# Top-k attention and an MLP on one core: values taken a step later and ahead of the scores, first MLP products four blocks to a PSUM bank

## The chip, the core and the metric

The kernel runs on one core of one Trainium2 chip. The metric is the device time of one execution in microseconds; the time before is 1606.17 us, the median of 3 runs (1605.85 to 1606.31). The engines are named as in the profile: PE (TensorE, matrix products), PEld (its weight loads), DVE (VectorE), ACT (ScalarE), POOL (GpSimd) and SP (SyncE, which issues the DMAs).

## The reference

```
# q, k, v: 8 batches, 8 heads, 576 rows, 64 columns, float32
scores = (q @ k.T) / sqrt(64)
kth = np.partition(scores, -32, axis=-1)[..., -32:-31]
scores = np.where(scores >= kth, scores, -1e9)
attn = softmax(scores)                       # 1e-9 is added to the sum
x = (attn @ v) laid out as (8 * 576, 8 * 64) # 4608 tokens x 512
h = x @ w_in                                 # 512 x 2048
g = h if h >= 1;  0 if h <= -1;  (h + 1)**2 / 4 between
out = g @ w_out                              # 2048 x 512
```

## The kernel before

**Tiles.** Attention goes in 144 steps. A step is 128 query rows of two heads: its scores are two tiles of 576 columns each. The 4608 tokens are 36 chunks of 128, and a chunk's 512 input columns (`xT`) are complete after four steps. The steps that hold the last 64 rows of two batches put four heads into one step.

**One step on the engines.** PE multiplies queries by keys (`scores`, L285), ACT copies the result to `s` (L287). DVE finds the 32nd largest of each row over several passes (`weights`, `first_top`, L297 to L388); ACT takes the exponential (L323); DVE masks and sums it (L386). POOL divides by the sum (`divide`, L339). In the late part of the kernel `move_w` (L412) then transposes the weights by DMA: ACT copies the 4-byte weights apart into 2-byte halves (L416), SP writes these to DRAM (L418) and reads them back with a transposing DMA (L419) into `wT`. PE multiplies `wT` by the values (`values`, L433 and L441), and ACT copies that product from PSUM into `xT` (L446, L448). In the first steps, while the MLP weights are still being converted (`convert_piece`), and in the last two, `transpose_w` (L395) does the transposing on PE instead, with a diagonal matrix `diag` that ACT makes.

**The MLP.** `mlp` cuts a chunk's work into items and appends them to the list `pending`. `hidden(x)` multiplies `GROUP` = 2 blocks of 128 hidden columns (16 matmul instructions) into one PSUM tile `ph`; ACT reads it twice (L470 to `r`, L477 to `g`), POOL makes the activation out of the two in three instructions (L482 to L484). `final(f)` adds one block's product with `w_out` to `py` (two instructions of 512 columns). The finals of a group come `LAG` = 4 groups behind its hidden item. After the last final ACT copies `py` to `y` (L492) and SP writes it out. The finals that are left over from a chunk are mixed between the first hidden items of the next.

**PSUM.** The tag `ph` has three buffers, shared by `ph` and the values' `po`; the tag `a` has two, shared by the scores `sp` and by all transposes (`pk`, `pq`, `pw`); `py` has one.

**The order.** PE, DVE, ACT and POOL each run their instructions in the order in which the program's planner emits them; SP's order isn't set by hand. The planner (L661 to L725) goes through the steps; step `m` has seven slots. In the late part, slot 0 emits the division of step `m-1`; slot 1 the transposes of queries and keys to come; slot 2 `move_w(m-1)`; slot 3 the maximum and first exponential of step `m+1` and a check of the MLP weights (`inspect`, ACT Sign); slot 4 the second exponential, `begin_at(m+2)` (the scores of step `m+2`) and `values_until(m-1)`, which is the values of step `m-2`. At the end of every slot `advance` takes items from `pending` as far as a budget `due` goes. An item costs one unit for each 128-column product of a hidden block (8 for a pair) and 4 for a final; the budget per step is `share`, about 32 units, and it is lowered so that the list doesn't run empty before the next chunk's values come (L669 to L673). An item whose weights aren't converted yet blocks the list.

Of the kernel before, what the change touches and what calls it, by code (L numbers as in the profile page):

```python
# [10 lines left out]
F32 = mybir.dt.float32  # L11
# [3 lines left out]
AF = mybir.ActivationFunctionType  # L15
ALU = mybir.AluOpType
# [8 lines left out]
def kernel(  # L25
# [10 lines left out]
    nc = tc.nc  # L36
    B, H, S, D = q.shape
# [13 lines left out]
    BANK = 512  # L51
    NK = DM // P
    NF = DFF // P
    GROUP = 2
    LAG = 4
    SCALE = float(D) ** -0.5

    const = ctx.enter_context(tc.tile_pool(name="const", bufs=1))
# [103 lines left out]

    def inspect_piece(pool, i):

        _, hi = words_of(pool, i, 2)
        for x in range(2):
            sign = pool.tile([P, WC], F32, name="sign", bufs=1)
            nc.scalar.activation(sign, hi.bitcast(F32), AF.Sign, bias=tiny[:, x:x + 1],  # L168
                                 accum_out=signs[:, x, i:i + 1])


    def run(ctx, paired):
# [24 lines left out]
        def load_queries(b, t):  # L197
            if t < NT:
                q_in = stage.tile([P, H, D], F32, name="q_in", bufs=2)
                nc.sync.dma_start(out=q_in, in_=whole(q, b)[:, :, t, :])  # L200
            else:
                q_in = stage.tile([TL, H, D], F32, name="q_tl", bufs=1)
                nc.sync.dma_start(out=q_in, in_=q[b, :, SM:S, :].rearrange("h p d -> p h d"))
            return q_in

# [124 lines left out]
        def divide(st):  # L330
            rz = att.tile([P, 2], F32, name="rz")
            nc.vector.reciprocal(rz, st["z"])
            if st["by_tensor"]:
                st["rz"] = diag = (late or words).tile([P, 2, P], F32, name="diag", bufs=1)
                for i in range(2):
                    nc.scalar.activation(diag[:, i, :], ident, AF.Copy, scale=rz[:, i:i + 1])
            else:
                for i in range(2):
                    nc.gpsimd.tensor_scalar(st["e"][:, i, :], st["e"][:, i, :], rz[:, i:i + 1], 1.0, ALU.mult, ALU.mult)  # L339
            if paired:  # L340
                m, seconds, kth = st["m"], st["seconds"], st["kth"]
                nc.gpsimd.tensor_tensor(out=excess[:, 2 * m:2 * m + 2], in0=seconds[:, 8:9 + SPLIT:SPLIT], in1=kth[:, LAST:7:-SPLIT],
                                        op=ALU.subtract)
# [50 lines left out]

        def transpose_w(st):  # L395
            w = st["e"]
            st["wT"] = wT = (late or words).tile([P, BLOCKS, P], F32, name="wT", bufs=2 if late else 1)
            pt = ps.tile([P, 2, NT, P], F32, name="pw", tag="a", bufs=2)
            for i in range(2):
                for c in range(NT):  # L400
                    nc.tensor.matmul(pt[:, i, c, :], w[:, i, main(i)][:, c * P:(c + 1) * P], st["rz"][:, i, :],  # L401
                                     start=True, stop=True)
            for i in range(2):
                nc.scalar.copy(wT[:, i * (NT + 1):i * (NT + 1) + NT], pt[:, i])
            pt = ps.tile([P, P], F32, name="pwt", tag="a", bufs=2)
            for i in range(2):
                nc.tensor.matmul(pt[i * TL:(i + 1) * TL, :], w[:, i, tail(i)], st["rz"][:, i, :], start=True, stop=True)
            nc.scalar.copy(wT[:, NT], pt)
# [1 line left out]


        def move_w(st):  # L412
            st["wT"] = wT = late.tile([P, BLOCKS, P], F32, name="wT", bufs=2)
            halves = late.tile([P, 2, 2 * S], U16, name="halves")
            for i in range(2):
                nc.scalar.copy(halves[:, :, i * S:(i + 1) * S], st["e"][:, i, :].bitcast(U16).rearrange("p (k t) -> p t k", t=2))  # L416
            rows = dram.tile([P, 2, 2 * S], U16, name="rows")
            nc.sync.dma_start(out=rows, in_=halves)  # L418
            nc.sync.dma_start_transpose(wT.bitcast(U16), rows.rearrange("p t k -> (p t) k"))  # L419
# [37 lines left out]
        def mlp(xT, rows, pool, last):  # L457
            gs, group = {}, 1 if last else GROUP
            py = []

            def hidden(x):
                ph = ps.tile([P, group, P], F32, name="ph", tag="ph", bufs=3)
                for i in range(group):
                    f = x * group + i
                    for kk in range(NK):
                        nc.tensor.matmul(ph[:, i], w_in[:, kk, f * P:(f + 1) * P], xT[:, kk],  # L466
                                         start=(kk == 0), stop=(kk == NK - 1))

                r = pool.tile([P, GROUP, P], F32, name="r", bufs=2)[:, 0:group]
                nc.scalar.activation(r, ph, AF.Relu, bias=half, scale=0.5)  # L470
                gs[x] = g = pool.tile([P, GROUP, P], F32, name="g", bufs=2 * LAG)[:, 0:group]
                if last:
                    nc.vector.tensor_scalar(g, ph, -1.0, 0.0, ALU.add, ALU.max)
                    nc.scalar.activation(r, r, AF.Square)
                    nc.vector.scalar_tensor_tensor(out=g, in0=r, scalar=1.0, in1=g, op0=ALU.min, op1=ALU.add)
                    return
                nc.scalar.activation(g, ph, AF.Relu, bias=minus, scale=1.0)  # L477
                if converted < n_pieces and x % 2:
                    nc.scalar.activation(r, r, AF.Square)
                    nc.gpsimd.tensor_scalar(r, r, 1.0, 0.0, ALU.min, ALU.max)  # L480
                else:
                    nc.gpsimd.tensor_scalar(r, r, 1.0, 0.0, ALU.min, ALU.max)  # L482
                    nc.gpsimd.tensor_tensor(out=r, in0=r, in1=r, op=ALU.mult)  # L483
                nc.gpsimd.tensor_tensor(out=g, in0=r, in1=g, op=ALU.add)  # L484

            def final(f):
                if f == 0:
                    py.append(ps.tile([P, DM], F32, name="py", tag="py", bufs=1))
                nc.tensor.matmul(py[0], gs[f // group][:, f % group], w_out[:, f, :], start=(f == 0), stop=(f == NF - 1))  # L489
                if f == NF - 1:  # L490
                    y = (late or words).tile([P, DM], F32, name="y", bufs=2)
                    nc.scalar.copy(y, py[0])  # L492
                    for p0, p1, dst in rows:
                        nc.sync.dma_start(out=dst, in_=y[p0:p1])

            behind = []
            while pending and pending[-1][3]:
                behind.insert(0, pending.pop())  # L500
            for x in range(NF // group + LAG):
                if x < NF // group:
                    pending.append((NK * group, needed(x * group + group - 1, False), partial(hidden, x), False))
                if x < LAG:
                    for _ in range(min(GROUP, len(behind))):
                        pending.append(behind.pop(0)[0:3] + (False,))
                else:
                    for f in range((x - LAG) * group, (x - LAG + 1) * group):
                        pending.append((DM // P, needed(f, True), partial(final, f), x >= NF // group))
# [151 lines left out]
        for m in range(n + 2):  # L661
# [6 lines left out]

            share, left = (total - spent) / (n + 2 - m), sum(x[0] for x in pending)  # L669
            for r in sorted(ready):  # L670
                if r + 3 > m and r >= valued:
                    share = min(share, left / (r + 3 - m))
                    left += NK * NF + NF * DM // P  # L673
            top_k, parts = None, [0] * SLOTS
            if m < n:
# [7 lines left out]
            for slot in range(SLOTS):  # L683
# [3 lines left out]
                if m < n and converted < n_pieces:  # L687
                    if slot in now_converting:
                        convert(now)
                elif slot == 3 and late is not None:  # L690
                    if m % 2:
                        inspect()
                    elif paired:
                        load(late, inspected, 2)
                if slot == 1 and 1 <= m <= n and state[m - 1]["by_tensor"]:
                    pe_time = max(pe_time, done[m - 1] + 2.0) + 1.0
                    transpose_w(state[m - 1])
                    ready_at[m - 1] = pe_time + 1.8
                if slot == 2 and 1 <= m <= n and not state[m - 1]["by_tensor"]:
                    move_w(state[m - 1])  # L700
                    ready_at[m - 1] = done[m - 1] + 14.0
                if slot == 2 and m == n and paired:
                    judge(ps, att)
                if slot == 2 and (early or m == first_late or m >= n - 1):
                    values_until(m)
                if m == 0 and slot in (1, 2):
                    next(first)
                if slot == 4:
                    begin_at(m + 2)
                    if not early:  # L710
                        values_until(m - 1)
                if slot == (6 if early else 1):
                    queries(m + 3)
                    if m < n and prep is None and next_keys < B and steps[m][0] == next_keys - 1 and steps[m][1] >= 1:
# [61 lines left out]
```

## Time and profile before

The profiled execution took 1610.32 us, and its span, from the first to the last instruction, is 1608.5 us: 1.8 us lie around the span. It is 4.15 us above the median of the three timed runs. The mean granted TensorE clock is 0.977.

| what | number |
|---|---|
| PE busy | 1514.0 us of 1608.5 |
| DVE busy | 1422.1 us (88%) |
| ACT busy | 1140.4 us (71%) |
| POOL busy | 943.3 us (59%) |
| hidden products, matmul instructions | 4608 |
| final products, matmul instructions | 1152 |
| reads of `ph` by ACT, 256 columns (L470, L477) | 280 + 280, 475 and 471 ns each |
| copies of `halves` by ACT (L416) | 260, 1153 ns each |
| transposing DMAs (L419) | 130 |

The engines work side by side, so only the time of the one that everything waits for can be taken off the end. The modelled ends of matmuls overlap the next one's start; how long a piece of PE work takes is therefore read from its start to the start of the piece behind it.

### The profile page before, as it was taken

What the parts mean: (1) busy time and instruction counts of PE and PEld (TensorE: products, weight loads), DVE (VectorE), ACT (ScalarE), POOL (GpSimd) and SP (SyncE); (2) the same over time, 40 slices, a digit from 0 to 9 for tenths busy, and PEclk for the clock granted to TensorE, in tenths of its full rate; (3) what the DMA queues carried; (4) which work ended last, traced back from release to release, by engine and by line L of the source; (5) the groups of instructions that cost most, each with busy time, mean ns of one, the idle gap of its engine ahead of it and who ended that gap; (6) DMA issues with size and microseconds to landing.
All of it is one profiled execution on the core that took longest, in us unless ns stands there. A gap on an engine that the chain in (4) does not pass through costs nothing.

```text
span 1608.5 us, 32395 instructions
## 1 busy us (share of the span) xinstructions
PE 1514.0 (94%) x10925; PEld 1080.7 (67%) x10925; DVE 1422.1 (88%) x4443; ACT 1140.4 (71%) x2308; POOL 943.3 (59%) x1376
## 2 busy tenths in 40 slices
PE   5587999999999999999999999999999999999988
PEld 4465676777667776777667767766666667666665
DVE  7999889999998998999999998999898998889932
ACT  5677567777777767777768877776677776677632
POOL 5766466666555665655556666555555665556640
PEclk7798999999999999999999999999999999999999
DMA  9433246565465556665565545655565555544410
GB/s 252 132 96 110 72 130 174 157 158 153 133 174 161 154 143 173 161 150 145 145 172 159 160 133 157 172 143 140 135 174 146 142 142 130 145 131 126 123 51 16
DMA packets 439056, 227.92 MB, mean 142 GB/s; under 512 B 393056, under 2 KB 401248, under 8 KB 438880
## 3 DMA queue, kind: packets, MB, share of 16 engines
q1 hardware_dynamic: 438880, 225.75, 51.8%
q8 instruction: 88, 1.44, 0.4%
q14 instruction: 88, 0.72, 0.1%
HBM read 62.91 MB, written 86.11 MB: 93 GB/s over the span
## 4 chain that ended last, share of the span: by engine, by line
PE 71%; ACT 13%; POOL 4%; DVE 4%; DMA 4%; issue 3%; SPq 1%; POOLq 0%; ACTq 0%; DVEq 0%
PE ph L466 27%; PE py L489 24%; PE sp L285 8%; PE po L433 7%; ACT halves L416 3%; ACT e L323 3%; DMA wT<-rows 2%; ACT s L287 2%; ACT sign L168 2%; PE pw L401 1%; POOL e L339 1%; POOL r L483 1%; PE po L441 1%; ACT r L470 1%; POOL g L484 1%
## 5 line engine op out<-in xcount | busy, mean ns | idle before, releaser
L466 PEld LDWEIGHTS ph<-xT,w_in 128*128 128x128 f32 x4608 | 554.4, 192 | 118.3 <-issue 79.8
L466 PE MATMUL ph<-xT,w_in 128*128 128x128 f32 x4608 | 576.1, 278 | 14.8 <-ACT xT L446 12.9
L489 PE MATMUL py<-w_out,g 128*128 128x512 f32 x1152 | 558.6, 601 | 7.3 <-ACT y L492 7.1
L482 POOL TENSOR_SCALAR r<-r 128x256 f32<-128x256 f32 x276 | 150.7, 546 | 526.5 <-ACT r L470 526.1
L307 DVE MATCH_REPLACE8 more<-tops,more 128x288 f32<-128x288 f32 x864 | 375.2, 437 | 0.0
L416 ACT COPY halves<-e 128x1152 uint16<-128x1152 uint16 x260 | 288.0, 1153 | 112.7 <-POOL e L339 111.5
L470 ACT ACTIVATE r<-ph,half 128x256 f32<-128x256 f32 (+1 forms) x296 | 139.0, 470 | 241.1 <-PE ph L466 227.9
L489 PEld LDWEIGHTS py<-w_out,g 128*128 128x128 f32 x1152 | 193.5, 191 | 137.0 <-issue 131.2
L386 DVE SCALAR_TENSOR_TENSOR e<-s,kth,e 128x577 f32<-128x577 f32 x288 | 249.2, 900 | 0.1
L484 POOL TENSOR_TENSOR g<-r,g 128x256 f32<-128x256 f32 x280 | 219.6, 784 | 22.0
L323 ACT ACTIVATE e<-s,nmax 128x576 f32<-128x576 f32 x288 | 217.4, 770 | 4.7
L339 POOL TENSOR_SCALAR e<-e,rz 128x576 f32<-128x576 f32 x260 | 218.6, 851 | 0.0
L483 POOL TENSOR_TENSOR r<-r 128x256 f32<-128x256 f32 x276 | 201.5, 730 | 23.0
L300 DVE TENSOR_TENSOR more<-s 128x576 f32<-128x576 f32 x144 | 114.9, 798 | 109.0 <-ACT s L287 108.6
L287 ACT ACTIVATE s<-sp 128x576 f32<-128x576 f32 x288 | 169.2, 638 | 4.5 <-PE sp L285 4.2
L285 PE MATMUL sp<-kT,qT 64*128 64x288 f32 x1024 | 162.0, 433 | 9.9 <-ACT kT L244 9.0
L285 PEld LDWEIGHTS sp<-kT,qT 64*128 64x128 f32 x1024 | 89.6, 188 | 98.9 <-issue 29.1
L433 PE MATMUL po<-wT,v_in 128*64 128x128 f32 x2048 | 145.9, 282 | 10.3 <-DMA wT<-rows 7.9
L433 PEld LDWEIGHTS po<-wT,v_in 128*64 128x64 f32 x2048 | 113.4, 139 | 60.5 <-issue 37.5
L477 ACT ACTIVATE g<-ph,minus 128x256 f32<-128x256 f32 x280 | 131.8, 471 | 0.0
L348 DVE MAX8 tops<-more 128x8 f32<-128x288 f32 x288 | 125.4, 442 | 0.0
L300 DVE TENSOR_TENSOR less<-s 128x576 f32<-128x576 f32 x144 | 117.4, 815 | 0.0
(92 smaller groups left out, 1528.2 us busy)
## 6 DMA issues: line engine op xcount, KB each, us to landing
rows<-halves SPq DMA_DIRECT2D x130, 576.0 KB, 2.8
raw<-in_moe_w_out_dram SPq DMA_DIRECT2D x52, 256.0 KB, 2.8
raw<-in_moe_w_in_dram SPq DMA_DIRECT2D x48, 256.0 KB, 2.9
k_in<-in_k_dram SPq DMA_DIRECT2D x64, 128.0 KB, 3.2
q_in<-in_q_dram SPq DMA_DIRECT2D x32, 256.0 KB, 3.3
v_in<-in_v_dram SPq DMA_DIRECT2D x8, 1024.0 KB, 5.9
out_dram<-y SPq DMA_DIRECT2D x32, 256.0 KB, 3.0
kT<-in_moe_w_in_dram SPq DMA_DIRECT2D x16, 256.0 KB, 4.6
```

The lines of the kernel that those rows point to most:

```text
L285: nc.tensor.matmul(o[:, a0 - c0:a1 - c0], qT[d, g, :], kT[d, g, k0:k0 + a1 - a0], start=True, stop=True)
L300: nc.vector.tensor_tensor(out=x, in0=s[:, :, 0:SH], in1=s[:, :, SH:S], op=op)
L307: nc.vector.match_replace(out=st["rest"][:, i, :], in_to_replace=eight(st["tops"], i, r - 8), in_values=src[:, i, :], imm_value=LOWEST)
L323: nc.scalar.activation(e[:, i, :], s[:, i, :], AF.Exp, bias=nmax[:, i:i + 1])
L339: nc.gpsimd.tensor_scalar(st["e"][:, i, :], st["e"][:, i, :], rz[:, i:i + 1], 1.0, ALU.mult, ALU.mult)
L386: nc.vector.scalar_tensor_tensor(out=st["all"][1][:, i, :], in0=st["all"][0][:, i, :], scalar=last[i], in1=st["all"][1][:, i, :], op0=ALU. ...
L416: nc.scalar.copy(halves[:, :, i * S:(i + 1) * S], st["e"][:, i, :].bitcast(U16).rearrange("p (k t) -> p t k", t=2))
L433: nc.tensor.matmul(po[j * D:(j + 1) * D], v_in[:, h, c, :] if c < NT else v_tl[0][:, h, :], wT[:, block(j, c)], start=(c == 0), stop=(c == ...
L466: nc.tensor.matmul(ph[:, i], w_in[:, kk, f * P:(f + 1) * P], xT[:, kk], start=(kk == 0), stop=(kk == NK - 1))
L483: nc.gpsimd.tensor_tensor(out=r, in0=r, in1=r, op=ALU.mult)
L484: nc.gpsimd.tensor_tensor(out=g, in0=r, in1=g, op=ALU.add)
L489: nc.tensor.matmul(py[0], gs[f // group][:, f % group], w_out[:, f, :], start=(f == 0), stop=(f == NF - 1))
```

## The change

The change has two parts and a number of smaller edits that fit them into the memory.

The first is in the MLP. `GROUP` becomes 4 and `LAG` 2: a hidden item is four blocks (16 units), its PSUM tile is a whole bank, and ACT reads it 512 columns at a time. POOL still works on 256 columns, in two rounds of three instructions. The list `pending` has half as many hidden items, each with the conversion of four blocks' weights as its condition.

The second is in the order. In the late part `begin_at(m+2)` goes from slot 4 to slot 2, and in front of it come the values of step `m-3` (`values_until(m-2)`). `move_w(m-1)` goes from slot 2 to slot 3. The planner's shares and due times are adapted (`r + 4`, 15.0), and `wT` has three buffers in place of two.

The smaller edits: the check of the weights writes its unused signs over the piece's low words, and its loads have one buffer; the 64-row queries share the buffers of the others; `diag` shares the tag of `halves`; `y` has one buffer in place of two.

```diff
-    GROUP = 2
-    LAG = 4
+    GROUP = 4
+    LAG = 2
...
-        _, hi = words_of(pool, i, 2)
+        lo, hi = words_of(pool, i, 1)
         for x in range(2):
-            sign = pool.tile([P, WC], F32, name="sign", bufs=1)
-            nc.scalar.activation(sign, hi.bitcast(F32), AF.Sign, bias=tiny[:, x:x + 1],
+            nc.scalar.activation(lo.bitcast(F32), hi.bitcast(F32), AF.Sign, bias=tiny[:, x:x + 1],
                                  accum_out=signs[:, x, i:i + 1])
...
-                q_in = stage.tile([TL, H, D], F32, name="q_tl", bufs=1)
+                q_in = stage.tile([TL, H, D], F32, name="q_tl", tag="q_in", bufs=2)
...
-                st["rz"] = diag = (late or words).tile([P, 2, P], F32, name="diag", bufs=1)
+                st["rz"] = diag = (late or words).tile([P, 2, P], F32, name="diag", tag="halves", bufs=1)
...
-            st["wT"] = wT = late.tile([P, BLOCKS, P], F32, name="wT", bufs=2)
+            st["wT"] = wT = late.tile([P, BLOCKS, P], F32, name="wT", bufs=3)
...
-                if converted < n_pieces and x % 2:
+                squared = converted < n_pieces and x % 2
+                if squared:
                     nc.scalar.activation(r, r, AF.Square)
-                    nc.gpsimd.tensor_scalar(r, r, 1.0, 0.0, ALU.min, ALU.max)
-                else:
-                    nc.gpsimd.tensor_scalar(r, r, 1.0, 0.0, ALU.min, ALU.max)
-                    nc.gpsimd.tensor_tensor(out=r, in0=r, in1=r, op=ALU.mult)
-                nc.gpsimd.tensor_tensor(out=g, in0=r, in1=g, op=ALU.add)
+                for c in range(0, group, 2):
+                    rh, gh = r[:, c:c + 2], g[:, c:c + 2]
+                    nc.gpsimd.tensor_scalar(rh, rh, 1.0, 0.0, ALU.min, ALU.max)
+                    if not squared:
+                        nc.gpsimd.tensor_tensor(out=rh, in0=rh, in1=rh, op=ALU.mult)
+                    nc.gpsimd.tensor_tensor(out=gh, in0=rh, in1=gh, op=ALU.add)
...
-                    y = (late or words).tile([P, DM], F32, name="y", bufs=2)
+                    y = (late or words).tile([P, DM], F32, name="y", bufs=1)
...
-                if r + 3 > m and r >= valued:
-                    share = min(share, left / (r + 3 - m))
+                if r + 4 > m and r >= valued:
+                    share = min(share, left / (r + 4 - m))
...
-                        load(late, inspected, 2)
+                        load(late, inspected, 1)
...
-                if slot == 2 and 1 <= m <= n and not state[m - 1]["by_tensor"]:
+                if slot == 3 and 1 <= m <= n and state[m - 1] is not None and not state[m - 1]["by_tensor"]:
                     move_w(state[m - 1])
-                    ready_at[m - 1] = done[m - 1] + 14.0
+                    ready_at[m - 1] = done[m - 1] + 15.0
...
-                if slot == 4:
+                if slot == 2 and not early:
+                    values_until(m - 2)
+                if slot == (4 if early else 2):
                     begin_at(m + 2)
-                    if not early:
-                        values_until(m - 1)
```

More of the change, by code (lines that the diff above doesn't have):

```diff
@@ L396, in transpose_w @@
             w = st["e"]
-            st["wT"] = wT = (late or words).tile([P, BLOCKS, P], F32, name="wT", bufs=2 if late else 1)
+            st["wT"] = wT = (late or words).tile([P, BLOCKS, P], F32, name="wT", bufs=3 if late else 1)
             pt = ps.tile([P, 2, NT, P], F32, name="pw", tag="a", bufs=2)
```

## The prediction

> **What bounds the kernel now.** First the page: busy times and the forty slices (40 us each).
>
> ```profile
> PE 1514.0 (94%) x10925; PEld 1080.7 (67%) x10925; DVE 1422.1 (88%) x4443; ACT 1140.4 (71%) x2308; POOL 943.3 (59%) x1376
> ...
> PE   5587999999999999999999999999999999999988
> DVE  7999889999998998999999998999898998889932
> ```
>
> PE is full from the fifth slice on, DVE nearly so before it. Which of the two sets the pace is told by who waits for whom (total us, times, longest), in the view of all waits:
>
> ```profile
> ACT halves L416 <- POOL e L339: 111.5, 59, 3.5
> DVE more L300 <- ACT s L287: 108.6, 89, 4.9
> ...
> PE ph L466 <- ACT xT L446: 12.9, 10, 2.2
> ...
> PE po L433 <- DMA wT<-rows: 7.9, 6, 3.5
> PE py L489 <- ACT y L492: 7.1, 6, 1.4
> ```
>
> DVE waits 108.6 us for scores, which come from PE's order. Its waits of this kind begin at 184 us, and DVE's shortest step is 9.17 us where the mean step between 183.8 and 1524.6 us is 1340.8/129 = 10.39. So DVE sets the pace up to about 184 us (steps 0 to 12, weight conversion), and PE from there on. Busy time by stretch (PE, PEld, DVE, ACT, POOL, granted clock, DMA):
>
> ```profile
> 183.80:985.60 801.80, 792.06 (x5804) 562.27 (x5803) 742.43 (x2329) 594.61 (x1174) 493.97 (x709) 1.00 0.57 154
> 985.60:1524.60 539.00, 518.70 (x3802) 365.02 (x3802) 489.70 (x1532) 389.71 (x763) 317.93 (x464) 1.00 0.53 143
> 1524.60:1608.50 83.90, 72.72 (x469) 52.99 (x464) 27.44 (x90) 29.37 (x75) 17.75 (x29) 0.96 0.13 39
> ```
>
> PE is idle for 9.7, 20.3 and 11.2 us, 41.2 in all. 6.3 of them are the last copy and its DMA; about 34 us can be had. Their names come from PE's own waits: xT 12.9 (L446) and 1.9 (L448); wT 10.8 (7.9, 2.1 at L441, 0.8 put down to ACT halves); y 7.1; one diag of 1.28 at 1539.6; 0.8 for the final check. That makes 34.8. What one xT wait is made of stands in the timeline at 1146 us (start, us, engine):
>
> ```profile
> 1146.15 1.09 PE L433 MATMUL po<-wT,v_in 128*64 128x128 f32 x16
> ...
> 1147.39 0.94 PE L466 MATMUL ph<-xT,w_in 128*128 128x128 f32 x6
> ...
> 1148.27 1.16 ACT L287 ACTIVATE s<-sp 128x576 f32<-128x576 f32 x2
> 1149.33 0.25 ACT L446 COPY xT<-po 128x128 f32<-128x128 f32 x1
> ...
> 1149.63 1.38 PE L466 MATMUL ph<-xT,w_in 128*128 128x128 f32 x10 [1.31 <-ACT xT L446]
> ```
>
> The values end and the new chunk's first hidden product follows at once. Its first six matmuls use older parts of xT; the seventh needs the copy, which stands on ACT behind two copies of scores.
>
> **The change part by part.**
>
> *Values in front of the scores.* Working the planner's shares and costs through for both orders, the first hidden item of a chunk follows its values with nothing between for 13 of the 31 middle chunks before, and after the change never with less than the scores between: 1.17 us, plus 0.67 for the six matmuls. ACT then has xT (0.26 us) in front of the copies of s. Of 14.8 us I keep 1.5 for late ACT: **-13.3**.
>
> *Values three steps old.* From move_w (slot 3 of step m) to its values (slot 2 of m+2) lie 13 slots; before, from slot 2 to slot 4 of the next step, it was 9. At 10.39 us per seven slots that is 19.3 instead of 13.4 us. The longest wT wait is 3.5 us, so 5.9 more covers each in the steady part. At the end step n-1 takes three values at once, the youngest with only six slots behind it; there I keep 1.5 of the 2.55 us at 1544.6. Of 10.8: **-9.3**. The diag wait goes too, since the last scores are emitted two slots earlier and PE has 16 us of items before that transpose, DVE 6: **-1.3**.
>
> *Four blocks to a bank.* On PE the same matmuls. y: between a chunk's last final and the next one's first lay as little as one pair, 1.79 us (the waits were up to 1.4 more); now it is at least one hidden item of four, 3.57. Of 7.1 I keep 1.0: **-6.1**. On ACT 128 columns cost 367 ns at L470 and 256 cost 475, or 0.84 ns a column (y's 512-column copy gives 0.84 too), so 512 cost about 0.69 us: 280 merges at 2 x 0.473 - 0.69 = 0.26 are 73 us of ACT. This lies beside PE and is worth nothing by itself. POOL has the same instructions (546, 730, 784 ns), in six pieces of 4.12 us in a row; the division behind them (0.85 each half) now comes 5.7 us after PE ends a hidden item. move_w stands a slot later and waits for it behind scores, nmax and an exponential, none of which needs it.
>
> *Here a rule speaks against the change.* The row first: ACT is 71% busy and its waits hold PE up for some 20 us (xT, y). The Trainium skill (Perfetto Trace Analysis, Optimizing Scalar/DVE Operations) says that where ACT isn't saturated but causes bubbles on other engines, breaking up instructions may let work finish sooner; this change merges them. By the rule each copy behind a pair of reads comes 2 x 0.21 us later, at 36 chunks up to 15 us lost. By the row what stands in front of xT in the new order is a hidden item that ended four finals (3.4 us) earlier, so nothing is lost. I take the row, and 15 us as the far end.
>
> *Order of shapes on PE.* Between 128-wide products and the half-array ones of scores and values there is a price: four finals take 1.72 us before a hidden item and 1.81 before scores; 16 hidden matmuls 1.79, behind values 1.88. Finals before values (1531.42 to 1533.23) are 1.81 as well, and finals behind scores 1.82 (181.90 to 183.72). Values to scores (180.41) shows no price, nor does scores to values. So 0.09 + 0.10 a step both before and after: 0. If the new order saves one, -12 (131 steps by 0.09), if it adds one, +12.
>
> *Added.* (1) A hidden item x needs 16x + 12 converted pieces where it needed 8x + 4, and it blocks the list. By the planner's count 264 units are pending at step 13 instead of 248; 16 units at 2 x 0.112 us are 3.6 us of PE work moved behind 184 us, where PE is full: **+3.6**, between 0 (PE catches up in its idle time) and 6 (scores held up by the longer item too). (2) Transposes of keys and queries stay in slot 1, now right in front of the scores, with the same two buffers of tag a: ACT must copy first (0.59 for queries, 2 x 0.58 for keys), while PE has values of 1.24 us between. 68 such places, most covered: **+2**, from 0 to 10. (3) SP: y's, raw's and the queries' DMAs have fewer buffers, each needed again a step or more later; wT's 5.9 us cover SP's order. The 32 units by which more is pending at the end (232 against 200) are the same PE work later: 0.
>
> *Sum.* -13.3 - 9.3 - 1.3 - 6.1 + 3.6 + 2 = **-24.4**. The profiled execution of 1610.32 (span 1608.5 and 1.8 around it) goes to 1585.9. It stood 4.15 over the median, so the median goes to 1581.8: **1582 us**. All 34 gone with nothing added gives 1572; half of the waits left and 10 added gives 1606 - 17 + 10 = 1599. That is the likeliest case's own range.
>
> **The rivals.** (A) *xT waits stay*, as ACT is late whatever its order: it has 8.3 us of work in a step of some 10 after the merge, and waits on POOL. For: 111.5 us of waits for the division today, and the longer pieces. Against: the 1.8 us of PE work now in front. 13.3 us come back: 1595. (B) *Slower: ACT and POOL become a loop that sets the pace.* Read r 0.69, POOL's six pieces 4.12, division 1.70, last half copy 1.15, exponential 0.77, together 8.4 us; then the next r. With the check (0.71 a step), key and query copies (0.44) and y (0.15) in series 9.7; with half of the scores' and xT's copies (0.78) 10.5. It decides from 10.39 us on, today's mean step; at 10.5 it costs 0.12 x 129 = 15 and nothing is won: about 1622. For: ACT and POOL are in order. Against: checks, scores and xT fit into ACT's wait for POOL. (C) *The gain is given back* through the early blocking, the shapes' prices and the bank of scores (6 + 12 + 10, against 30): 1604 to 1606.
>
> **Chances.** Forecast 0.67, A 0.16, B 0.12, C 0.05. A measurement tells a change from none at about 0.2% (3.2 us). Faster 0.83, same 0.04, slower 0.13. The range runs from 1570, just below the best sum, to 1602: B and most of C are left out, and the small part of the likeliest that falls outside.
>
> **What will show it.** PE's waits for xT, wT and y should fall from 34 us to under 8 together; PE's idle from 184 us to the last product to under 12, and the step in that stretch to about 10.2. L470 and L477 should show 512 columns near 0.69 us with half the count. DVE's waits for s stay, for PE still leads. New PE rows "sp <- ACT kT" or "qT" above 5 us would be (2) mis-sized; step 12's end later than 184 us would be (1). PE idle in front of ph for ACT r or g, with ACT waiting for POOL e, would be B, and the forecast wrong.

## The result, and the profile after

The changed kernel takes 1593.28 us, the median of 4 runs (1592.51 to 1593.85), beside 1606.24 us for the kernel before, timed with it: a ratio of 0.9915 (95% interval 0.9897 to 0.9932). It is faster by 13 us where 24 were forecast. The profiled execution took 1592.51 us with a span of 1590.7; against the profiled execution of before the span is 17.8 us shorter. The two counts differ by some 5 us, because the profiled execution of before lay 4.1 us above its median and that of the changed kernel 0.8 below.

Busy time of each engine on the page:

```profile
PE 1510.2 (95%) x10925; PEld 1079.9 (68%) x10925; DVE 1429.8 (90%) x4443; ACT 1109.1 (70%) x2026; POOL 976.9 (61%) x1376
```

By stretch, with the same cuts as before (length, then PE, PEld, DVE, ACT and POOL busy, granted clock, DMA):

```profile
183.80:985.60 801.80, 794.37 (x5812) 564.18 (x5814) 759.50 (x2357) 580.68 (x1023) 509.34 (x710) 1.00 0.57 153
985.60:1524.60 539.00, 536.08 (x3994) 380.53 (x3990) 503.99 (x1578) 389.71 (x681) 347.80 (x478) 1.00 0.56 149
1524.60:1590.70 66.10, 54.90 (x302) 37.58 (x301) 10.33 (x35) 18.45 (x47) 10.46 (x19) 0.97 0.04 15
```

PE's idle time in these three is 7.4, 2.9 and 11.2 us, 21.5 where it was 41.2. In front of 183.8 us it is 80.5 - 21.5 = 59.0 us where it was 94.5 - 41.2 = 53.3. So 19.7 us are won behind the start, 5.7 are lost in it, and PE's busy time is 3.8 us shorter, which no run explains: 17.8 in all. What PE waited for behind 184 us (total, times, longest), from its own waits:

```profile
PE po L432 <- DMA wT<-rows: 5.6, 4, 4.1
PE pw L400 <- ACT diag L335: 3.2, 2, 1.6
PE py L490 <- ACT y L493: 2.4, 4, 0.9
```

The waits for xT (14.8 us) are gone, and y's fell from 7.1 to 2.4. wT's fell only from 10.8 to 5.6, and the diag waits at the end rose from 1.3 to 3.2. In the view of all waits ACT shows what has become of its place in the order; the first line is of the kernel before, the others of the changed one:

```profile
ACT xT L446 <- PE po L433: 8.1, 6, 4.1
...
ACT xT L445 <- PE po L432: 141.3, 97, 4.2
...
DVE more L299 <- ACT s L286: 52.3, 70, 2.2
...
ACT halves L415 <- POOL e L338: 32.1, 38, 3.0
```

ACT now waits for the values to be done in 97 places, where it did so in 6, and PE no longer waits for the copy; and the 111.5 us for POOL's division have become 32.1. The group rows by shape give the wide read and the division:

```profile
L338 POOL TENSOR_SCALAR e<-e,rz 128x576 f32<-128x576 f32 x260 | 289.9, 1124 | 1.2 <-DVE rz L331 1.2
...
L469 ACT ACTIVATE r<-ph,half 128x512 f32<-128x512 f32 x140 | 94.8, 677 | 104.4 <-PE ph L465 104.2
```

The 512-column read takes 677 ns (0.69 was estimated). Of the other signs that the prediction named, two were just missed: the waits for xT, wT and y are 8.0 us together (under 8 was named), and PE's idle time from 184 us to its last product is 13.3 us (under 12). The mean step is 10.1 us (10.2).

### The profile page after: what moved, and what is told of

Same layout as the page of the kernel before. It is cut to its first block, busy times and chain, and to the rows that moved or that the text cites. A ratio compares the mean times of both kernels' runs of the same rounds, so it can differ in the third digit from the quotient of the medians.

```text
span 1590.7 us, 31863 instructions
## 1 busy us (share of the span) xinstructions
PE 1510.2 (95%) x10925; PEld 1079.9 (68%) x10925; DVE 1429.8 (90%) x4443; ACT 1109.1 (70%) x2026; POOL 976.9 (61%) x1376
## 4 chain that ended last, share of the span: by engine, by line
PE 84%; ACT 6%; POOL 3%; DVE 3%; DMA 3%; issue 2%; POOLq 0%; ACTq 0%; DVEq 0%; SPq 0%
PE ph L465 31%; PE py L490 29%; PE sp L284 10%; PE po L432 9%; ACT halves L415 1%; PE pw L400 1%; PE po L440 1%; DMA wT<-rows 1%; PE pq L263 1%; DMA rows<-halves 1%; ACT e L322 1%; PE pk L239 1%; POOL e L338 1%; POOL g L485 1%; ACT s L286 1%
## 5 line engine op out<-in xcount | busy, mean ns | idle before, releaser
L465 PEld LDWEIGHTS ph<-xT,w_in 128*128 128x128 f32 x4608 | 533.6, 192 | 64.3 <-issue 61.0
L465 PE MATMUL ph<-xT,w_in 128*128 128x128 f32 x4608 | 548.4, 277 | 0.0
L490 PE MATMUL py<-w_out,g 128*128 128x512 f32 x1152 | 541.8, 600 | 2.5 <-ACT y L493 2.4
L490 PEld LDWEIGHTS py<-w_out,g 128*128 128x128 f32 x1152 | 200.8, 191 | 191.6 <-issue 179.4
L415 ACT COPY halves<-e 128x1152 uint16<-128x1152 uint16 x260 | 287.2, 1145 | 33.7 <-POOL e L338 32.1
L338 POOL TENSOR_SCALAR e<-e,rz 128x576 f32<-128x576 f32 x260 | 289.9, 1124 | 1.2 <-DVE rz L331 1.2
L385 DVE SCALAR_TENSOR_TENSOR e<-s,kth,e 128x577 f32<-128x577 f32 x288 | 245.1, 883 | 12.4 <-ACT e L322 12.2
L322 ACT ACTIVATE e<-s,nmax 128x576 f32<-128x576 f32 x288 | 222.8, 774 | 4.7
L484 POOL TENSOR_TENSOR r<-r 128x256 f32<-128x256 f32 x276 | 186.7, 677 | 23.0
L469 ACT ACTIVATE r<-ph,half 128x512 f32<-128x512 f32 (+1 forms) x156 | 100.7, 646 | 125.0 <-PE ph L465 124.8
L299 DVE TENSOR_TENSOR more<-s 128x576 f32<-128x576 f32 x144 | 131.0, 910 | 53.0 <-ACT s L286 52.3
L432 PEld LDWEIGHTS po<-wT,v_in 128*64 128x64 f32 x2048 | 114.2, 139 | 87.0 <-issue 57.9
L432 PE MATMUL po<-wT,v_in 128*64 128x128 f32 x2048 | 147.1, 284 | 9.5 <-DMA wT<-rows 5.6
L445 ACT COPY xT<-po 128x128 f32<-128x128 f32 x128 | 33.7, 263 | 141.7 <-PE po L432 141.3
L299 DVE TENSOR_TENSOR less<-s 128x576 f32<-128x576 f32 x144 | 116.5, 809 | 0.0
```

The lines of the kernel that those rows point to most:

```text
L299: nc.vector.tensor_tensor(out=x, in0=s[:, :, 0:SH], in1=s[:, :, SH:S], op=op)
L322: nc.scalar.activation(e[:, i, :], s[:, i, :], AF.Exp, bias=nmax[:, i:i + 1])
L385: nc.vector.scalar_tensor_tensor(out=st["all"][1][:, i, :], in0=st["all"][0][:, i, :], scalar=last[i], in1=st["all"][1][:, i, :], op0=ALU. ...
L432: nc.tensor.matmul(po[j * D:(j + 1) * D], v_in[:, h, c, :] if c < NT else v_tl[0][:, h, :], wT[:, block(j, c)], start=(c == 0), stop=(c == ...
```

## The experiments

The theory was the prediction's: the new order wins what is won, groups of four cost something at the start, and ACT's busy time is worth nothing. The rival was that the wide reads, which relieve ACT, are the gain. A summary first; ratios are to the kernel before, timed with each, and the last column is PE's idle time before 184 us.

| kernel | median us | ratio, 95% interval | PE idle to 184 us |
|---|---|---|---|
| changed kernel | 1593.28 | 0.9915, 0.9897 to 0.9932 | 59.2 |
| order_only | 1582.46 | 0.9842, 0.9826 to 0.9859 | 55.7 |
| group_only | 1750.20 | 1.0882, 1.0863 to 1.0902 | 59.9 |
| narrow_reads | 1589.88 | 0.9884, 0.9864 to 0.9904 | 59.5 |
| early_pairs | 1574.06 | 0.9782, 0.9763 to 0.9801 | 53.5 |
| move_ahead | 1648.66 | 1.0252, 1.0235 to 1.0270 | 60.1 |
| diag_own | 1593.57 | 0.9913, 0.9897 to 0.9928 | 60.4 |
| combined | 1663.51 | 1.0340, 1.0318 to 1.0363 | 55.1 |
| hold_hidden | 1579.37 | 0.9818, 0.9805 to 0.9831 | 57.9 |
| pairs_y | 1568.34 | 0.9748, 0.9734 to 0.9761 | 54.7 |
| group_move3 | 1703.20 | 1.0594, 1.0577 to 1.0611 | 60.2 |
| values_behind | 1589.21 | 0.9877, 0.9858 to 0.9897 | 55.7 |
| fours_best | 1571.83 | 0.9769, 0.9752 to 0.9785 | 55.0 |

### The order alone

```diff
-    GROUP = 4
-    LAG = 2
+    GROUP = 2
+    LAG = 4
```

> The changed kernel with GROUP 2 and LAG 4 as before, so only the order is new. Theory (the gain is the order: PE no longer waits for xT): PE's waits for xT stay under 1 us, those for y come back to 4 to 7 us, the 6 us lost before 184 us are not lost; 1588 to 1594 us, about the changed kernel. Rival (the gain is the 512-column reads, which relieve ACT): nearly all of it is gone, 1603 us or more.

It took 1582.46 us. The rival falls: the order without the wide reads wins 26 us, twice what the whole change does. The time is below the theory's 1588 too, so groups of four cost 11 us more than they bring. PE's waits behind 184 us:

```profile
PE py L490 <- ACT y L493: 12.2, 11, 2.5
PE po L432 <- DMA wT<-rows: 1.5, 2, 1.0
```

No xT wait is left, and y's are 12.2 us, more than the 4 to 7 expected. The waits for wT are under 2. The smaller edits stay in this kernel, `wT`'s third buffer among them; no run takes that buffer away, so what it adds to the order isn't known.

### Groups of four alone

```diff
-                if slot == 3 and 1 <= m <= n and state[m - 1] is not None and not state[m - 1]["by_tensor"]:
+                if slot == 2 and 1 <= m <= n and not state[m - 1]["by_tensor"]:
...
-                if slot == 2 and not early:
-                    values_until(m - 2)
-                if slot == (4 if early else 2):
+                if slot == 4:
                     begin_at(m + 2)
+                    if not early:
+                        values_until(m - 1)
```

The other two edits put back `r + 3` and 14.0.

> The changed kernel with the order of before (slots 2 and 4, r + 3, due time 14), so only the groups of four are new. Theory: the xT waits are back at 10 us or more, y's are under 3, the 6 us of the start are lost; 1603 to 1611 us. Rival (wide reads are the gain): 1590 to 1596 us.

1750.20 us: both missed, by far more than anything in the prediction. The view of all waits of this kernel, behind 184 us:

```profile
ACT halves L415 <- POOL e L338: 324.1, 86, 5.1
...
PE po L432 <- DMA wT<-rows: 73.4, 37, 4.3
```

In the old order the copies of halves come in slot 2, and POOL's division stands behind six pieces instead of three. ACT waits 324 us for it, wT is late 37 times at L432, and PE's granted clock falls to a mean of 0.952. Groups of four need something of the new order; they were not an addition to it.

### Which part of the order they need

> group_only, but move_w in slot 3 and due time 15 as in the change; scores and values stay in slot 4 in the old order. Theory (in group_only ACT's copies in slot 2 wait for POOL's division, which stands behind six pieces, and the reads of the next hidden item wait behind them: a loop of ACT and POOL): ACT's waits for POOL e fall from 324 us to under 120 and the time from 1750 to between 1600 and 1660 us, the rest being waits for xT and wT. Rival (groups of four fail in the old order because values come too early for them): 1700 us or more.

The edit against group_only:

```diff
-                if slot == 2 and 1 <= m <= n and not state[m - 1]["by_tensor"]:
+                if slot == 3 and 1 <= m <= n and state[m - 1] is not None and not state[m - 1]["by_tensor"]:
                     move_w(state[m - 1])
-                    ready_at[m - 1] = done[m - 1] + 14.0
+                    ready_at[m - 1] = done[m - 1] + 15.0
```

1703.20 us. ACT's waits for the division fell to 137.6 us and 47 us were won, but PE still waits 63.2 us for wT at L432 and 14.5 at L440. So the place of move_w is worth 47 us of the 157 between group_only and the changed kernel. The theory had put most of it there; the rival's mark, 1700 us or more, was met. The larger part is the rest of the order, scores and values in slot 2 with the values three steps old. The late wT points to the age of the values, but no run separates it from the slot.

### The reads alone

```diff
-                nc.scalar.activation(r, ph, AF.Relu, bias=half, scale=0.5)
+                cuts = [(c, min(c + 2, group)) for c in range(0, group, 2)]
+                for c0, c1 in cuts:
+                    nc.scalar.activation(r[:, c0:c1], ph[:, c0:c1], AF.Relu, bias=half, scale=0.5)
...
-                nc.scalar.activation(g, ph, AF.Relu, bias=minus, scale=1.0)
+                for c0, c1 in cuts:
+                    nc.scalar.activation(g[:, c0:c1], ph[:, c0:c1], AF.Relu, bias=minus, scale=1.0)
```

> The changed kernel, but ACT reads each bank in two instructions of 256 columns where it reads it in one of 512. Theory (ACT's busy time isn't on the path): ACT's busy time is some 60 to 75 us longer, the time within 3 us of the changed kernel's 1593. Rival (wide reads are the gain): 1600 us or more. By the rule that smaller instructions let work finish sooner: below 1590 us.

ACT is busy for 1148.2 us instead of 1109.1, and the time is 1589.88. That is at the edge of what the rule of smaller instructions asked for (below 1590), and the interval of its ratio just touches the changed kernel's: a small gain of the narrow reads is neither shown nor ruled out. The rival's 1600 is out: 39 us of ACT work saved win nothing here. They are fewer than the 60 to 75 expected, for each of the 280 reads more added 0.14 us to the busy time and not 0.26.

### The start

```diff
-            gs, group = {}, 1 if last else GROUP
+            gs, group = {}, 1 if last else 2 if converted < n_pieces else GROUP
```

> The changed kernel, but chunks that enter the list while weights are still being converted are cut into pairs as before. Theory (blocks of four cost about 6 us at the start): step 11 ends near 171 us where it ended at 177, and the time falls to 1586 to 1589 us. Rival (the start is caught up later): within 2 us of 1593.

Step 11 ended at 172.9 us instead of 177.3, and PE's idle time before 184 us is back at 53.5. But the time fell by 19 us to 1574.06, three times the expected amount. Something else had changed.

### Where the hidden item stands

In early_pairs no wait for wT is left. The changed kernel's longest is 4.05 us, and the timeline shows how it comes about. A row that ends in x2 or more merges that many instructions.

```profile
806.13 0.69 ACT L469 ACTIVATE r<-ph,half 128x512 f32<-128x512 f32 x1 [3.11 <-PE ph L465]
...
809.36 2.19 ACT L415 COPY halves<-e 128x1152 uint16<-128x1152 uint16 x2
809.46 1.10 PE L432 MATMUL po<-wT,v_in 128*64 128x128 f32 x16
...
811.58 0.54 SPq L417 DMA_DIRECT2D rows<-halves  x1
...
818.52 2.44 SPq L418 DMA_TRANSPOSE wT<-rows  x1
...
823.20 1.98 PE L432 MATMUL po<-wT,v_in 128*64 128x128 f32 x16 [4.05 <-DMA wT<-rows]
```

ACT copies the halves at 809.36, and the values that need them are the next but one in PE's order: those at 809.46 are already running, so those due at 819.15 (823.20 - 4.05). That is 9.8 us, not the 19.3 of the prediction. In this stretch the planner puts the hidden item into slot 2, in front of move_w in slot 3; so ACT waits 3.11 us for PE to end it, reads it, and then takes nmax, an exponential and a check before the halves. A 1 MB load of values (issued at 810.59) stands in front of rows, issued at 811.58, and the transposing DMA follows only at 818.52: 6.9 us, where the step before took 4.1 (799.94 to 804.00). By this estimate the load made up 2.9 of the 4.05 us of waiting, and the slot left no slack to take them. In early_pairs the same load is issued at 808.99:

```profile
810.26 3.84 PE L465 MATMUL ph<-xT,w_in 128*128 128x128 f32 x32
...
812.47 2.37 ACT L415 COPY halves<-e 128x1152 uint16<-128x1152 uint16 x2 [0.48 <-POOL e L338]
...
815.42 0.67 ACT L469 ACTIVATE r<-ph,half 128x512 f32<-128x512 f32 x1
...
827.09 1.09 PE L432 MATMUL po<-wT,v_in 128*64 128x128 f32 x16
```

Here the halves go in front of the read, while PE works on the hidden item, and the values that need them start at 827.09, 14.6 us later, without a wait. The planner's budget of some 32 units a step isn't exactly the work of a step, so the slot of the hidden item can drift through the step, and the different start of early_pairs can have shifted the drift. Two experiments tell this from the start.

```diff
-                if slot == 3 and 1 <= m <= n and state[m - 1] is not None and not state[m - 1]["by_tensor"]:
-                    move_w(state[m - 1])
-                    ready_at[m - 1] = done[m - 1] + 15.0
...
                 if slot == (4 if early else 2):
                     begin_at(m + 2)
+                if slot == 2 and 1 <= m <= n and state[m - 1] is not None and not state[m - 1]["by_tensor"]:
+                    move_w(state[m - 1])
+                    ready_at[m - 1] = done[m - 1] + 15.0
```

> The changed kernel, but move_w(m-1) is emitted in slot 2 right behind the scores, in front of the hidden item that advance puts there, so that ACT's halves don't stand behind the reads of a hidden item PE hasn't done. Theory (the wT waits that are left come from ACT's order, not from the three steps): halves start 2 to 4 us earlier against the values that use them, the waits of PE for wT in the steady part (4.9 us) fall under 1, and the time by 3 to 6 us to 1587 to 1590. Rival (a 1 MB load of values holds up the DMAs, wherever the halves stand): a wait of 2 us or more for wT stays and the time is within 2 us of 1593.

1648.66 us, slower than the kernel before: a miss of 60 us for theory and rival alike. The wT waits are gone as expected, but the prediction's rival B has come true. Timeline of one step of this kernel:

```profile
440.82 0.67 ACT L469 ACTIVATE r<-ph,half 128x512 f32<-128x512 f32 x1
...
441.58 0.45 POOL L482 TENSOR_SCALAR r<-r 128x256 f32<-128x256 f32 x1 [4.76 <-ACT r L469]
...
445.39 2.56 POOL L338 TENSOR_SCALAR e<-e,rz 128x576 f32<-128x576 f32 x2
...
447.26 2.21 ACT L415 COPY halves<-e 128x1152 uint16<-128x1152 uint16 x2 [3.70 <-POOL e L338]
...
449.61 1.44 ACT L322 ACTIVATE e<-s,nmax 128x576 f32<-128x576 f32 x2
...
450.95 0.67 ACT L469 ACTIVATE r<-ph,half 128x512 f32<-128x512 f32 x1
```

Each row waits for the one above it: read, six pieces on POOL, division, halves, exponentials, the next read. From read to read it is 10.1 us here and 10.6 in the mean between steps 12 and 141, more than the 10.39 us from which the prediction had rival B decide. Moving halves forward for every step closes the loop that slot 3 had left open.

```diff
                 if due < cost or pe_time >= until:
                     break
+                if cost == NK * GROUP and late is not None and slot in (1, 2) and m < n:
+                    break
```

> The changed kernel with blocks of four from the start, but the planner holds a hidden item back in slots 1 and 2 until slot 3, so that in the late part it never stands in front of move_w on ACT. Theory (of the 19 us that early_pairs won, some 6 are the start and the rest is that its hidden items never stand in slot 1 or 2, so that wT is in time): the wT waits and the slow clock behind them go, the start stays slow (step 11 ends near 177 us), 1582 to 1587 us. Rival (early_pairs won everything at the start): within 3 us of 1593.

1579.37 us, 14 below the changed kernel, with the start as slow as in it (step 11 ends at 177.7). So the place of the hidden item is the larger of the two losses, and larger than expected. In its profile the waits for wT between 500 and 1000 us (5.0) and the slow clock behind them (3.4, see the last section) are gone, and PE is idle for 1.3 us less between 184 and 500 us and 1.3 less before; about 3 us of the 14 have no name. One wait for wT of 2.1 us stays near the end. Both mends together:

> The changed kernel with both mends: pairs while weights are converted, and no hidden item of four in slots 1 and 2. Theory (start and place in the step are two losses that overlap: early_pairs had moved the items out of slots 1 and 2 too): PE's waits behind 184 us stay under 6 us and the time is 1570 to 1575 us, not below pairs_y's 1568. Rival (groups of four have a gain of their own, hidden so far): below 1565 us.

1571.83 us. Against hold_hidden that is 7.5 us for the start alone. The time is that of early_pairs (1574.06) within overlapping intervals, as the theory said: early_pairs had moved the item out of slots 1 and 2 by accident, and so had both mends.

### The shared buffer, and all at once

```diff
-                st["rz"] = diag = (late or words).tile([P, 2, P], F32, name="diag", tag="halves", bufs=1)
+                st["rz"] = diag = (late or words).tile([P, 2, P], F32, name="diag", bufs=1)
```

> The changed kernel, but diag has a buffer of its own again and doesn't share the tag of halves. Theory (the two last transposes wait for the DMA out of halves through the shared buffer): the waits of PE for diag behind 1500 us (3.2 us in two) fall under 2, the time by 1 to 3 us. Rival (they wait for DVE): no difference.

1593.57 us, no difference, and the diag waits at the end are 2.5 us. The shared tag isn't worth any time.

The last kernel of this kind has this edit, move_ahead's and early_pairs' together.

> Pairs while weights are converted, move_w in slot 2 behind the scores, and diag with its own buffer, all in the changed kernel. Theory (three separate losses, which add): 6 + 4 + 2 = 12 us less than the changed kernel, 1579 to 1584 us. Rival (one of them covers for another, or PE is full): 1586 us or more.

1663.51 us. It contains move_ahead, and that decides. It is 15 us slower than move_ahead alone, though early_pairs by itself had won 19; no run explains this.

### What pairs can do, and what the place of the values is worth

```diff
-                    for _ in range(min(GROUP, len(behind))):
+                    for _ in range(min(GROUP + 1, len(behind))):
```

This is order_only with one edit.

> order_only (pairs, new order), but the finals left over from a chunk are mixed in three to a hidden item, so that two hidden items lie between the last of them and the new chunk's first final. Theory (what pairs still lose in the new order is the y wait, 12 us in one profile): y waits under 3 us, 1570 to 1577 us, no slower than groups of four ever were. Rival (fours have a gain of their own on PE or ACT): 1580 us or more.

1568.34 us, the fastest of all, 2.5% below the kernel before. PE's waits behind 184 us:

```profile
PE po L432 <- DMA wT<-rows: 1.2, 2, 0.7
PE py L490 <- ACT y L493: 0.8, 1, 0.8
```

The y wait was all that pairs still lost, and one more final between two hidden items mends it. Groups of four in their best form stay 3.5 us above, with intervals that overlap; no gain of their own was found.

```diff
+                if slot == (4 if early else 2):
+                    begin_at(m + 2)
                 if slot == 2 and not early:
                     values_until(m - 2)
-                if slot == (4 if early else 2):
-                    begin_at(m + 2)
```

This too is order_only with one edit.

> order_only (pairs, new order), but in slot 2 the scores stand in front of the values, which stay three steps old. Theory (the place in front of the scores is what hides xT's copy): PE's waits for xT come back to 8 us or more, wT's stay under 3, the time is 1588 to 1596 us against order_only's 1582. Rival (the age of the values and the slot are what counts): xT waits under 3 us, within 3 us of 1582.

1589.21 us, the time that the theory gave, but for another reason. No wait for xT came back at all. What PE waits for now, besides y (10.6 us), is the keys:

```profile
PE sp L284 <- ACT kT L243: 4.0, 4, 1.3
```

So, with pairs at least, the scores behind the values aren't what removed the xT waits. These went with slot 2 in place of 4, move_w in slot 3 and the age of the values, which put ACT's exponentials, checks and halves behind xT's copy; this reading is argued, and no run takes the three apart. The place of the values is worth some 7 us of its own: 4 of them are the waits for keys, which ACT now copies right before the scores; the other 3 have no name.

## Why the prediction was right, and where its sizes were off

The time lies in the range, 1570 to 1602, and the kernel became faster; but half of the expected gain is missing: 13 us of 24. Of the 11 us that are missing, 6.6 are missing in the profiles (17.8 where the sum was 24.4) and 4.8 come from the frame.

**What bounds the kernel** held. PE sets the pace behind 184 us in both kernels, and the waits named there were the gain: PE's idle time behind it fell by 19.7 us.

**Values in front of the scores, -13.3:** the size was right (-14.8), the reason only in part. The prediction counted on PE's 1.17 us of scores between; values_behind takes these away and no xT wait comes back. ACT's order is what is left as the reason; it is argued, not shown.

**Values three steps old, -9.3:** the step that failed. The working counted 13 slots, 19.3 us, from move_w to the values as the planner emits them. ACT doesn't copy the halves there: where a hidden item stands in slot 1 or 2, its read comes first and waits for PE, and at the longest wait it was 9.8 us from the halves to the values. wT waits fell by 5.2 us instead of 9.3. The longest drew slow clock after it, but two waits of the kernel before had drawn as much (half of 2.81 and 3.41 us of PE's work against half of 3.41 and 2.88, see the last section), so in the difference of the two kernels the clock cancels. hold_hidden, which changes only the place of the hidden item, won 14 us.

**The diag wait, -1.3:** wrong in sign, +1.9, and in diag_own, without the shared buffer, 2.5 us remain and the time is the same. The trace of the changed kernel names what came last:

```profile
1512.89 0.17 DVE L331 RECIPROCAL rz<-z 128x2 f32<-128x2 f32 x1
1513.11 0.69 ACT L335 ACTIVATE diag<-ident,rz 128x128 f32<-128x128 f32 x2 [1.08 <-DVE rz L331]
...
1524.73 0.69 ACT L469 ACTIVATE r<-ph,half 128x512 f32<-128x512 f32 x1 [4.36 <-PE ph L465]
1525.32 0.68 ACT L476 ACTIVATE g<-ph,minus 128x512 f32<-128x512 f32 x1
1525.89 0.69 ACT L335 ACTIVATE diag<-ident,rz 128x128 f32<-128x128 f32 x2
```

The first diag waits for DVE's sums. The second has them (the reciprocal at 1512.89 is the last of its line) and stands in ACT's order behind the reads of a hidden item that PE has only just ended. It is the step of wT over again: an engine in order, held by a read in front.

**y, -6.1:** -4.7. **The wide reads, 0:** they win nothing, by narrow_reads. The rule that smaller instructions let work finish sooner was given a far end of 15 us of loss; the run with smaller ones is 3 us faster by the medians, with intervals that just touch. The row was near enough, but whether the rule holds for a few us stays open.

**Shapes on PE, 0:** right. In both kernels four finals take 1.72 us before a hidden item and 1.81 before the first half-array product, and the way back costs 0.10.

**The start, +3.6:** too small: 5.7 in the profiles, and 7.5 between hold_hidden and fours_best. The 16 units were counted as work that moves. DVE's step 11 also ended 5.9 us later (171.4 to 177.3); the prediction's own bound of 6 had named the reason, scores held up by the longer item, but no run separates it.

**The bank of scores, +2:** small, as said: behind 184 us PE waits 0.2 us for a query copy in front of scores, and 0.8 for a copy in front of a key transpose.

**Rival B** (ACT and POOL as a loop) was put at 8.4 us in the step of the changed kernel and does not decide there; in move_ahead it does. The forecast's margin was one place in ACT's order.

**The frame** took 4.15 us off both sides. This assumed that the waits of before are as long in the median execution as in the profiled one. The spans differ by 17.8 us and the medians by 13.0: the profiled execution of before lay 4.1 us above its median and that of the changed kernel 0.8 below, so 4.8 us of what was counted as a gain were not there in the medians.

## What to carry to other kernels

Measure the slack of a transfer from where its engine really issues its source to where the user starts, in the timeline, and not in slots of the program: an in-order engine that must first read a product which isn't finished moves everything behind it. When the work of an engine that isn't the bound is made coarser, look for a chain through several in-order engines that closes on itself, and add up its length, for it is short of deciding by one place in the order. Before a change of two parts is kept, run each alone: here one part won 26 us and the other gave 11 of them back.

## What was not expected of the hardware

The clock after a wait. The granted clock in these traces changes at steps of 3.41 us. Windows cut at these steps around the same place in the two kernels, of the kernel before (length; busy time of PE, PEld, DVE, ACT and POOL; granted clock, DMA share, GB/s):

```profile
816.98:820.39 3.41, 1.74 (x10) 0.69 (x8) 3.41 (x12) 1.58 (x2) 2.60 (x5) 1.00 1.19 278
820.39:823.81 3.42, 1.57 (x21) 1.40 (x22) 3.42 (x15) 3.39 (x8) 1.75 (x3) 1.00 0.91 258
823.81:827.22 3.41, 3.41 (x21) 2.48 (x20) 3.41 (x9) 1.52 (x5) 0.22 (x1) 1.00 0.23 75
```

and of the changed one:

```profile
819.18:822.60 3.42, 0.00 (x0) 0.00 (x0) 3.42 (x10) 2.28 (x3) 3.26 (x6) 1.00 0.87 208
822.60:826.01 3.41, 2.81 (x22) 2.51 (x24) 3.41 (x15) 0.27 (x1) 1.28 (x2) 0.50 0.38 149
826.01:829.42 3.41, 3.41 (x16) 2.37 (x15) 1.19 (x3) 1.30 (x2) 0.00 (x0) 0.50 0.83 162
```

PE's idle time of 3.52 us up to 822.24 in the kernel before left the clock at 1.00; the one of 4.05 us in the changed kernel was followed by 6.8 us at half. Over 820 to 840 us the mean is 0.83, which is 3.4 us lost, nearly as much again as the wait. But the length of the wait isn't what decides. In the kernel before, a wait of 1.86 us (for xT, up to 1402.61) and one of 2.55 (for wT, up to 1544.56) stand in these windows:

```profile
1400.69:1404.10 3.41, 1.55 (x14) 1.49 (x14) 2.65 (x8) 1.87 (x4) 0.00 (x0) 1.00 0.62 172
1404.10:1407.51 3.41, 3.41 (x7) 1.35 (x6) 3.41 (x12) 0.86 (x3) 2.52 (x5) 0.50 0.46 103
...
1540.61:1544.03 3.42, 1.40 (x14) 1.03 (x12) 1.24 (x4) 1.24 (x3) 1.28 (x2) 1.00 0.81 173
1544.03:1547.44 3.41, 2.88 (x28) 2.91 (x30) 0.00 (x0) 0.27 (x1) 0.00 (x0) 0.50 0.00 0
```

Both shorter waits drew half clock, for the first lay in one window and the second with 2.0 us of its length, while the wait of 3.52 us was divided between two. In the traces of all 14 kernels, behind 184 us, a window at full clock in which PE was busy for less than 45% was followed by half clock in 72 cases of 72; between 45 and 50% in 5 of 19; above 50% in 2 of 5673. The Trainium skill (TensorE: Matmul & The Clock Gate, Part 1) gives a window of 3413 ns that runs freely, which agrees, and has the clock fall after an idle window; here it fell behind windows in which PE had worked for up to nearly half of the time, and the measurement decides.

POOL's division, the same 260 instructions on the same shape, took 851 ns each before, 1124 in the changed kernel, 907 in order_only and 886 in pairs_y. Two of the changed kernel, and DVE beside them:

```profile
713.34 2.73 POOL L338 TENSOR_SCALAR e<-e,rz 128x576 f32<-128x576 f32 x2
...
714.05 0.74 DVE L299 TENSOR_TENSOR more<-s 128x576 f32<-128x576 f32 x1
714.71 0.74 DVE L299 TENSOR_TENSOR less<-s 128x576 f32<-128x576 f32 x1
```

The first of the two ends as DVE's pair of tensor-tensor instructions starts and takes 0.74 us; the second, which lies beside them, takes 2.00. So it is throughout: in the changed kernel the 92 divisions that share no more than 0.05 us with DVE's L299 or L385 (the instructions with two tensors as input) take 0.73 to 0.75 us, and the 168 others up to 2.04; in the kernel before (L300 and L386) 139 took 0.74 to 0.76 us, and the 121 others up to 1.97. The order decides what POOL's division meets on DVE. How much of the 1124 ns reaches the end of the kernel no run shows.
